# A feed-forward block and a long convolution on one core: which activation pairs take the seven-product path in both matrix products, when their buffers are lent, and how long the planner takes adding transfers to be

## The chip, the cores and the metric

The kernel runs on one core of one Trainium2 chip. The time is the device time of one execution in microseconds (us); the figure given for a kernel is the median of its runs. The engines of the core are PE (TensorE, matrix products), DVE (VectorE), ACT (ScalarE), POOL (GpSimd, here almost only an issuer of adding transfers) and SP (SyncE, which issues the other transfers). Each engine works through its own queue of instructions in the order in which they were written.

## The reference

Two branches read the same layer-normalised rows and are added to the input (S = 2048 rows, D = 1024, F = 3584; all float32):

```python
xn = _layernorm(x, axis=-1)                                  # x = A_q
# branch A: short causal convolution of k (4 taps), times v, then a long causal convolution by FFT
kv = k_shift * v
y  = irfft(rfft(pad(kv)) * rfft(pad(ssm_k)))[:S] + kv * ssm_D
A  = xn * y
# branch B: feed-forward
B  = silu(xn @ w1) @ w2
out = x + A + B
```

## The kernel before

Branch B is what PE mostly does. Each float32 factor is split into a high and a low float16 part and each product of blocks is made of three matmuls (high by high, high by low, low by high; lines 916 to 918 for the first matrix product, 1046 to 1048 for the second). The 3584 hidden columns are 28 blocks of 128, or 14 pairs (`NP`).

The first matrix product (`units`, line 952) uses a Strassen-Winograd scheme: for a pair and one half of the rows, seven products P1 to P7 of 12 matmuls take the place of eight. Such a unit is 84 matmuls. The first row half (`sp` = 0) has units for pairs 2 to 13, the second (`sp` = 1) for pairs 0 to 13; pairs 0 and 1 are done in plain form for the first half, before the units. PE shares four accumulators (`ff`) with the engines that empty them: in `evacuate` (line 879) PE has to wait until ACT has copied a running sum (P6 waits for the copy of P1's sum, P5 for that of P6's, P3 for that of P5's), and until DVE has added two of them into the low half (the two `v_tt` there, line 336 in the profile, `hf<-ff,hf`).

What follows on a unit depends on the pair. For the pairs that are not in `PAIRS`, `blocks` (line 841) splits the activation of each of two row blocks into float16 parts (one ACT and one DVE instruction of 1024 columns for each) and stores four transfers of 256 KB in `hs`. For the four pairs in `PAIRS`, `quad` (line 799) makes the seven sums and differences that the second matrix product needs for its own seven-product scheme: four `v_tt` of 512 columns on DVE, three splits of 1024 columns and one of 512 (ACT and DVE both), and seven stores of 256 KB in `hsf`. The split tiles live in `hts`, two tiles that can each be halved. The unsplit upper half of such a pair lives in `parts`, two places in the buffer `x4` that are kept until the row half's last quad is done (`room`, line 831).

The second matrix product adds up the ten plain pairs (`steps2`, for all 16 row tiles and two column halves, 1920 matmuls) and then the four pairs of `PAIRS` in `units2` (672 matmuls). Each result is copied or combined into a tile of `hfs` and sent out by POOL with a transfer that adds to `out` in memory (`G`, line 331).

Branch A, the convolution, goes on under all this in eight groups of 128 channels: DVE does most of it (a radix step, the product in the frequency domain, the inverse step; tiles `spec` and `tmp`), and once a group PE has a burst of 96 matmuls (tiles `ps`, lines 1494 to 1496 forward and 1686 to 1688 inverse). The result of a burst is gated into `yt` (or into `hts` or `wo` tiles), which POOL adds to `out` with `G`.

The order of the instructions on all engines is made by a list scheduler inside the kernel (`Order`, line 106). Each stream of work is a generator of `Op`s; each `Op` has an estimate `busy` of the time it holds its engine and `late` of the time until its result can be used. The scheduler always emits the op that can start first by these estimates, less a bias for its stream. For `G` the estimate is 1.1 us on POOL and 3.0 us more until the transfer has landed, which is when the tile it reads may be written again.

Once `flag["quads", 1]` is set (the second half's last quad has its last split), the `hts` tiles are not needed by branch B any more, and the convolution's streams may take them as further buffers (`parts_tile`, `signal_parts`, `parts_of`, `norm_rows`, `gated`).

Of the kernel before, what the change touches and what calls it, by code (L numbers as in the profile page):

```python
# [18 lines left out]
ADD, SUB, MUL = ALU.add, ALU.subtract, ALU.mult  # L19
# [10 lines left out]
NP = NF // 2  # L30
# [9 lines left out]
            "P5": ("S1", "T1"), "P3": ("S4", "B22"), "P4": ("A22", "T4")}  # L40
XPLACE = dict(A11=2, A12=3, A22=5, S1=0, S2=6, S3=7, S4=1)

PAIRS = (10, 11, 12, 13)
NQ = len(PAIRS)
PLAIN = [j for j in range(NF) if j // 2 not in PAIRS]
NC = len(PLAIN) // 4
# [59 lines left out]
class Order:  # L106
# [27 lines left out]
    def add(self, gen, bias, floor=0.0):  # L134
        s = Stream(gen, bias, floor)
        self.streams.append(s)
        self.advance(s)
# [151 lines left out]
def h3_ffn_kernel(ctx, tc, x, kp, vs, fs, shift, dskip, w1, w2, cfwd, cinv, out):  # L289
    nc = tc.nc  # L290
    ctx.enter_context(tc.manual_schedule())
    order = Order()
    add = order.add
    flag = defaultdict(Token)
# [12 lines left out]
    def size(a):  # L307
        n = 1
        for s in a.shape[1:]:
            n *= s  # L310
        return n
# [10 lines left out]
    def L(o, i, m=0.3):  # L322
        n = size(o) * o.shape[0] * mybir.dt.size(o.dtype)
        return Op("SP", 0.4, 0.1, lambda: nc.sync.dma_start(o, i), [i], [o], m, n)
# [5 lines left out]

    def G(o, i, m=0.3):
        n = size(i) * i.shape[0] * mybir.dt.size(i.dtype)
        return Op("POOL", 1.1, 3.0, lambda: nc.gpsimd.dma_start(o, i, accum_op=ADD), [i], [o], m, n)  # L333

    def v_tt(o, a, b, op, **k):
        return V(lambda: nc.vector.tensor_tensor(o, a, b, op=op), o, [a, b], **k)  # L336
# [20 lines left out]
    def split(hi, lo, src, scale, after=()):  # L357

        yield a_act(hi, src, AF.Copy, scale)
        yield v_stt(lo, src, scale, hi, MUL, SUB)  # L360
        for t in after:
            t.set()
# [39 lines left out]
    wo = Halves(order, wp, "wo", WO)  # L402
    hfs = Halves(order, wp, "hf", 3)
    vs_r = ws_r = hfs
    hts = Halves(order, wp, "ht", 2)
# [391 lines left out]
    quads = defaultdict(dict)  # L797

    def quad(i, sp):

        def factors(names, hf, toks=()):
            n = len(names)
            yield hts.ready if n == 1 else hts.pairs
            ht, ttok = (hts.tile if n == 1 else hts.pair)([P, 4 * n, 2, P], F16, n)
            yield from split(ht[:, :, 0], ht[:, :, 1], hf, wsc[:, i, 2:3], toks)
            for f, name in enumerate(names):
                yield L(hsf[sp][name][:, :, PAIRS.index(i)].rearrange("q p h s -> p q (h s)"),
                        ht[:, 4 * f:4 * f + 4].rearrange("p q h s -> p q (h s)"))
                ttok.set()

        yield flag["quad", i, 2 * sp]
        up, utok = quads[i, 2 * sp]
        flat = [up.rearrange("p j q s -> p (j q) s")]
        yield from factors(("A11", "A12"), flat[0])
        yield flag["quad", i, 2 * sp + 1]
        low, ltok = quads[i, 2 * sp + 1]
        flat.append(low.rearrange("p j q s -> p (j q) s"))
        x, y, z, v = up[:, 0], up[:, 1], low[:, 0], low[:, 1]
        yield from factors(("A22",), flat[1][:, 4:])
        yield v_tt(v, z, v, ADD)  # L820
        yield v_tt(z, x, z, SUB)
        add(factors(("S3", "S1"), flat[1], (ltok,)), 0.1)
        yield v_tt(x, v, x, SUB)
        ltok.set()
        yield v_tt(y, y, x, SUB)
        add(factors(("S2", "S4"), flat[0], (utok, flag["quads", sp])), 0.1)

    for sp in range(2):
        flag["quads", sp] = Token(NQ)

    def room():

        for sp in range(2):
            yield flag["room", sp]
            yield places[4].ready
            t, tok = places[4].tile([P, 2, 2 * W], F32)
            parts.open(t, 2)
            yield flag["quads", sp]
            tok.set()

    def blocks(i, b, hf, tok, ready):

        if i in PAIRS:
            return
        for r in ready:
            yield r
        yield hts.pairs
        ht, ttok = hts.pair([P, 8, 2, P], F16, 2)
        yield from split(ht[:, :, 0], ht[:, :, 1], hf.rearrange("p j q s -> p (j q) s"), wsc[:, i, 1:2], (tok,))
        for j in range(2):  # L850
            yield L(hs[b][:, :, 2 * i + j].rearrange("q p h s -> p q (h s)"),
                    ht[:, 4 * j:4 * j + 4].rearrange("p q h s -> p q (h s)"))
            ttok.set()

    def silu(i, o, src, tok, done):
        yield a_act(o, src, AF.Silu, wsc[:, i, 3:4])
# [6 lines left out]
    def places_of(i, b):  # L863

        made = Token(2)
        if i in PAIRS:
            r = hfs if b % 2 else parts
# [84 lines left out]
    def units():  # L952
# [5 lines left out]
        for n, (i, sp) in enumerate(todo):  # L958
            if sp == 1:
                flag["unit", i].set()  # L960
                flag["room", 1].set()
            if i in PAIRS:
                add(quad(i, sp), 0.1)
# [361 lines left out]
    def convolution(floor):  # L1325
# [3 lines left out]
        sp = ra.tile([P, 2, 8, 2, 2 * P], F32, name="spec")  # L1329

        def ring(name, bufs, pool=ra):
            return Ring(order, pool, name, bufs)

        kin_r, kf_r, acc_r, cm_r = (ring(*a) for a in (
            ("kin", 1), ("kf", 1), ("acc", 1), ("cm", 1)))
        hl_r = Halves(order, ra, "hl", 3)
# [90 lines left out]
        def parts_tile(hr, lr):  # L1427

            two = []
            for r in (hr, lr):  # L1430
                yield lambda: r.ready() or flag["quads", 1]() and hts.ready()
                two.append((r if r.ready() else hts).tile([P, 2, 2 * 2 * P], F16))
            return two

        def signal_parts():

            for g in range(NG):
                yield flag["scales", g]
                acc, atok = accs[g]
                for t in TO:  # L1440
                    yield lambda: cm_r.ready() or flag["quads", 1]() and hts.ready()
                    c, ctok = cpart[g, t] = (cm_r if cm_r.ready() else hts).tile([P, 2, 4, P], F16)
                    yield from split(c[:, 0], c[:, 1], slots(acc)[:, t::4], scs[g][0][:, 0:1], (flag["cpart", g, t],))
                atok.set()

        def parts_of():

            for g in range(NG):
                yield flag["scales", g]
                kf, ktok = kfs[g]  # L1450
                for t in TO:
                    yield lambda: hl_r.pairs() or flag["quads", 1]() and hts.pairs()
                    part[g, t] = x, _ = (hl_r if hl_r.pairs() else hts).pair([P, 2, 2, 4, P], F16)
                    done = flag["part", g, t]
                    done.n = 2
                    add(split(x[:, 1, 0], x[:, 1, 1], slots(kf)[:, t::4], scs[g][0][:, 1:2], (ktok, done)), CB)
                    yield flag["cpart", g, t]
                    c, ctok = cpart.pop((g, t))
                    yield X(x[:, 0].rearrange("p f s w -> p (f s) w"), c.rearrange("p f s w -> p (f s w)"))
                    ctok.set()  # L1460
                    done.set()
# [195 lines left out]
        def norm_rows():  # L1657

            for g in range(NG):
                for t in TO:  # L1660
                    r = more["xg"]
                    yield lambda: r.ready() or flag["quads", 1]() and hts.ready()
                    xgs[g, t] = xg, _ = (r if r.ready() else hts).tile([P, 2, 2, P])
                    for b in range(2):
                        yield L(xg[:, b], x4[b][:, :, t, g * P:(g + 1) * P])
                    for b in range(2):
                        for i in range(2):
                            n = b * T2 + 4 * i + t
                            yield a_act(xg[:, b, i], xg[:, b, i], AF.Identity, rstd[:, n:n + 1], nmr[:, n:n + 1])
                    flag["xg", g, t].set()  # L1670
# [23 lines left out]
        def gated(g, t, py, tok):  # L1694
            yield flag["xg", g, t]
            xg, xtok = xgs.pop((g, t))
            r = more["yt"]
            yield lambda: r.ready() or flag["quads", 1]() and hts.ready() or flag["h end"]() and wo.ready()
            r = wo if flag["h end"]() and wo.ready() else r if r.ready() else hts
            yt, ytok = r.tile([P, 2, 2, P], uses=2)  # L1700
            sc, stok = scs[g]
            flat = [q.rearrange("p b i w -> p (b i w)") for q in (yt, py, xg)]
            yield v_stt(flat[0], flat[1], sc[:, 5:6], flat[2], MUL, MUL)
            tok.set()
            xtok.set()
            if t == TO[-1]:
                stok.set()
            yield flag["copied", g // (NG // 2)]
            for b in range(2):
                yield G(out4[b][:, :, t, g * P:(g + 1) * P], yt[:, b])  # L1710
                ytok.set()
                if g < NG // 2:
                    flag["conv out"].set()
# [108 lines left out]
```

## Time and profile before

| | |
|---|---|
| median of 3 runs | 1261.48 us (1260.78 to 1261.53) |
| the profiled execution, its time | 1262.56 us |
| the profiled execution, its span | 1260.8 us |
| granted TensorE clock, mean | 0.992 |
| instructions in the span | 17032 |

The profile shows one execution. A row of a group reads: line, engine, operation, what it writes from what it reads (buffer numbers left out), shapes, how often, then busy time and mean duration, then how long the engine stood idle just before these instructions and which instruction ended that. A row of the timeline reads: start and duration in us, engine, line, operation, and in brackets the idle time before it with the instruction that ended it. In a row of a stretch stand its length and then, for each engine, the busy time and the number of instructions, then the granted clock, the mean busy share of the 16 transfer engines and the rate in GB/s.

### The profile page before, as it was taken

The page shows a single profiled execution, that of the slowest core. Times are in us where ns is not written, and L with a number is a line of the kernel's source. Part 1 is how long each engine was busy: PE and PEld are TensorE (multiplying, and loading weights), DVE is VectorE, ACT ScalarE, POOL GpSimd, SP SyncE. Part 2 cuts the span into 40 slices and gives each one's busy share as a digit, 9 for nine tenths or more (in the row PEclk, how much of TensorE's full clock was granted, in tenths as well). Part 3 has the DMA queues.
Part 4 walks back from the last instruction along what each step waited for, and adds up shares of the span by engine and source line. Part 5 has one row for each costly group of instructions (what it writes and reads, how often), then busy time and mean ns, then how long its engine had stood idle before and what let it go on. Part 6 is the DMA issues. An engine that isn't in the chain of part 4 may idle for free.

```text
span 1260.8 us, 17032 instructions
## 1 busy us (share of the span) xinstructions
PE 1233.3 (98%) x6018; PEld 596.5 (47%) x6018; DVE 1148.6 (91%) x1515; ACT 731.0 (58%) x1169; POOL 132.8 (11%) x141
## 2 busy tenths in 40 slices
PE   7899999999999999999999999999999999999997
PEld 6444554444444454444444544544444454445444
DVE  7999997898799979999999899989979989998995
ACT  6858897877866686667762442372263246536232
POOL 0000000000000030001110210120030021113114
PEclk7999999999999999999999999999999999999999
DMA  9358889879999799889998797599477578977767
GB/s 333 93 173 275 285 301 327 271 253 328 329 346 297 252 242 283 243 248 271 335 334 210 175 263 182 136 273 255 117 160 208 138 158 239 273 162 139 157 139 92
DMA packets 254181, 292.93 MB, mean 232 GB/s; under 512 B 48784, under 2 KB 167568, under 8 KB 251920
## 3 DMA queue, kind: packets, MB, share of 16 engines
q1 hardware_dynamic: 227360, 266.93, 67.9%
q0 software_dynamic: 26736, 24.92, 14.8%
q8 instruction: 47, 0.77, 0.2%
q14 instruction: 38, 0.31, 0.1%
HBM read 193.22 MB, written 98.57 MB: 231 GB/s over the span
## 4 chain that ended last, share of the span: by engine, by line
PE 63%; DVE 18%; DMA 3%; issue 3%; ACT 3%; POOL 0%; DVEq 0%; ACTq 0%
PE ff L1046 9%; PE ff L1048 9%; PE ff L1047 9%; PE ff L916 9%; PE ff L918 9%; PE ff L917 9%; DVE spec L336 7%; DVE tmp L336 3%; PE ps L1494 2%; PE ps L1496 2%; PE ps L1495 2%; DVE x L339 1%; DVE ht L339 1%; DVE acc L339 1%; DVE hf L336 1%
## 5 line engine op out<-in xcount | busy, mean ns | idle before, releaser
L1046 PE MATMUL ff<-x,wo 128*128 128x512 f16 x864 | 327.4, 379 | 1.2 <-ACT hf L347 0.8
L1048 PE MATMUL ff<-x,wo 128*128 128x512 f16 x864 | 327.4, 379 | 0.0
L1047 PE MATMUL ff<-x,wo 128*128 128x512 f16 x864 | 327.4, 379 | 0.0
L916 PE MATMUL ff<-x,wo 128*128 128x512 f16 (+1 forms) x808 | 305.6, 378 | 6.4 <-ACT x L347 2.2
L917 PE MATMUL ff<-x,wo 128*128 128x512 f16 (+1 forms) x808 | 305.4, 378 | 2.2 <-DVE x L339 2.2
L918 PE MATMUL ff<-x,wo 128*128 128x512 f16 (+1 forms) x808 | 305.5, 378 | 1.6 <-DVE wo L339 1.6
L336 DVE TENSOR_TENSOR spec<-spec 128x1024 f32<-128x1024 f32 (+2 forms) x272 | 263.5, 1000 | 2.8
L1048 PEld LDWEIGHTS <-wo 128*128 128x128 f16 x864 | 84.5, 98 | 101.9
L1046 PEld LDWEIGHTS <-wo 128*128 128x128 f16 x864 | 85.5, 99 | 99.5
L1047 PEld LDWEIGHTS <-wo 128*128 128x128 f16 x864 | 84.5, 98 | 101.2 <-issue 1.8
L918 PEld LDWEIGHTS <-wo 128*128 128x128 f16 x808 | 79.9, 99 | 98.0 <-issue 3.4
L917 PEld LDWEIGHTS <-wo 128*128 128x128 f16 x808 | 79.9, 99 | 95.2 <-issue 7.4
L916 PEld LDWEIGHTS <-wo 128*128 128x128 f16 x808 | 81.3, 101 | 89.3 <-ACT wo L347 1.0
L333 POOL DMA_DIRECT2D out<-hf x63 | 57.5, 917 | 458.8 <-ACT hf L347 402.9
L333 POOL DMA_DIRECT2D out<-yt x56 | 62.5, 1275 | 330.6 <-DVE yt L339 188.3
L347 ACT ACTIVATE hf<-ff,invc 128x512 f32<-128x512 f32 x64 | 43.4, 681 | 91.9 <-PE ff L1048 68.9
L336 DVE TENSOR_TENSOR tmp<-spec 128x2048 f32<-128x2048 f32 (+1 forms) x48 | 92.2, 1934 | 1.0
L347 ACT ACTIVATE spec<-spec 128x1024 bf16<-128x1024 f32 x32 | 33.8, 1055 | 92.4 <-DVE spec L336 92.4
L339 DVE SCALAR_TENSOR_TENSOR ht<-hf,wsc,ht 128x1024 f16<-128x1024 f32 (+1 forms) x56 | 67.3, 1203 | 10.9 <-ACT ht L347 10.9
L339 DVE SCALAR_TENSOR_TENSOR acc<-kin,taps,acc 128x1024 f32<-128x1024 f32 x48 | 61.5, 1280 | 11.9 <-ACT acc L347 11.6
L347 ACT ACTIVATE spec<-ps 128x512 f32<-128x512 f32 x96 | 54.9, 590 | 19.0 <-PE ps L1496 17.7
L347 ACT ACTIVATE ht<-hf,wsc 128x1024 f16<-128x1024 f32 (+1 forms) x56 | 60.9, 1088 | 5.0 <-DVE hf L336 1.4
(168 smaller groups left out, 1743.1 us busy)
## 6 DMA issues: line engine op xcount, KB each, us to landing
wo<-hs SPq DMA_DIRECT2D x160, 256.0 KB, 3.9
hs<-ht SPq DMA_DIRECT2D x80, 256.0 KB, 4.7
out<-hf POOLq DMA_DIRECT2D x63, 256.0 KB, 4.5
wraw<-in_w SPq DMA_DIRECT2D x30, 512.0 KB, 5.6
raw<-in_w SPq DMA_DIRECT2D x28, 512.0 KB, 5.5
kin<-in_kp SPq DMA_DIRECT2D x16, 704.0 KB, 6.1
kf<-in_fs SPq DMA_DIRECT2D x8, 1024.0 KB, 5.8
hl<-in_vs SPq DMA_DIRECT2D x32, 256.0 KB, 5.7
```

The costliest lines, as they stand in the source:

```text
L333: return Op("POOL", 1.1, 3.0, lambda: nc.gpsimd.dma_start(o, i, accum_op=ADD), [i], [o], m, n)
L336: return V(lambda: nc.vector.tensor_tensor(o, a, b, op=op), o, [a, b], **k)
L339: return V(lambda: nc.vector.scalar_tensor_tensor(o, a, s, b, op0=op0, op1=op1), o, [a, b] + ([] if isinstance(s, float) else [s]), **k)
L347: nc.scalar.activation(o, i, func, scale=scale, **kw)
L916: nc.tensor.matmul(o, w[:, 0, k], xf[:, :, k, 0], start=first and k == 0, stop=False, **kw)
L917: nc.tensor.matmul(o, w[:, 0, k], xf[:, :, k, 1], start=False, stop=False, **kw)
L918: nc.tensor.matmul(o, w[:, 1, k], xf[:, :, k, 0], start=False, stop=last and k == KH - 1, **kw)
L1046: nc.tensor.matmul(po, hx[:, n, 0, :], wc[:, n, 0, :], start=first and n == 0, stop=False, **kw)
L1047: nc.tensor.matmul(po, hx[:, n, 0, :], wc[:, n, 1, :], start=False, stop=False, **kw)
L1048: nc.tensor.matmul(po, hx[:, n, 1, :], wc[:, n, 0, :], start=False, stop=last and n == 3, **kw)
L1494: nc.tensor.matmul(o, cf[:, 0], hi[i], start=i == 0, stop=False, **kw)
L1495: nc.tensor.matmul(o, cf[:, 0], lo[i], start=False, stop=False, **kw)
```

## The change

Three edits. `PAIRS` becomes (8, 9, 12, 13), so pairs 8 and 9 take the seven-product path in both matrix products and pairs 10 and 11 go the plain way; `PLAIN` follows from it, and the fifth group of plain blocks in the second matrix product is pairs 10 and 11. A new token `flag["activations"]` counts every quad and every plain block (`2 * NQ + 4 * (NP - NQ)` of them); the five places that lent `hts` tiles on `flag["quads", 1]` wait for it. The estimate `late` of `G` goes from 3.0 to 4.8 us; it is a number of the planner and no instruction has it.

```diff
-PAIRS = (10, 11, 12, 13)
+PAIRS = (8, 9, 12, 13)
...
-        return Op("POOL", 1.1, 3.0, lambda: nc.gpsimd.dma_start(o, i, accum_op=ADD), [i], [o], m, n)
+        return Op("POOL", 1.1, 4.8, lambda: nc.gpsimd.dma_start(o, i, accum_op=ADD), [i], [o], m, n)
...
-        add(factors(("S2", "S4"), flat[0], (utok, flag["quads", sp])), 0.1)
+        add(factors(("S2", "S4"), flat[0], (utok, flag["quads", sp], flag["activations"])), 0.1)
...
+    flag["activations"] = Token(2 * NQ + 4 * (NP - NQ))
...
             ttok.set()
+        flag["activations"].set()
...
-                yield lambda: r.ready() or flag["quads", 1]() and hts.ready()
+                yield lambda: r.ready() or flag["activations"]() and hts.ready()
...
-                    yield lambda: cm_r.ready() or flag["quads", 1]() and hts.ready()
+                    yield lambda: cm_r.ready() or flag["activations"]() and hts.ready()
...
-                    yield lambda: hl_r.pairs() or flag["quads", 1]() and hts.pairs()
+                    yield lambda: hl_r.pairs() or flag["activations"]() and hts.pairs()
...
-                    yield lambda: r.ready() or flag["quads", 1]() and hts.ready()
+                    yield lambda: r.ready() or flag["activations"]() and hts.ready()
...
-            yield lambda: r.ready() or flag["quads", 1]() and hts.ready() or flag["h end"]() and wo.ready()
+            yield lambda: r.ready() or flag["activations"]() and hts.ready() or flag["h end"]() and wo.ready()
```

## The prediction

> **What bounds the kernel now.** The page's first part is read first, for the engine that could set the end.
>
> ```profile
> span 1260.8 us, 17032 instructions
> PE 1233.3 (98%) x6018; PEld 596.5 (47%) x6018; DVE 1148.6 (91%) x1515; ACT 731.0 (58%) x1169; POOL 132.8 (11%) x141
> ```
>
> PE is busy for 98% of the span, but a busy PE need not be at its pace, so the timeline comes next, where PE goes on after a stop.
>
> ```profile
> 589.85 0.38 PE L916 MATMUL ff<-x,wo 128*128 128x512 f16 x1 [2.02 <-ACT hf L347]
> ...
> 590.50 0.38 PE L916 MATMUL ff<-x,wo 128*128 128x512 f16 x1
> ```
>
> Two matmuls are left out between these, so the starts are 0.216 us apart (0.65 over three) although one lasts 0.38. Matmuls follow at this pace wherever nothing is waited for, so a unit of 84 takes 18.1 us, and the change leaves all of them in place. Only PE's stops can therefore be won or lost. The view of stretches of 30 us says where they are (the second number of a row is PE busy), and the view of waits says on whom.
>
> ```profile
> 0.00:30.00 30.00, 21.42 (x134) 17.93 (x135) 21.99 (x61) 17.93 (x40) 0.70 (x6) 0.81 0.96 347
> 30.00:60.00 30.00, 25.42 (x140) 14.56 (x139) 28.59 (x56) 27.68 (x45) 0.00 (x0) 0.90 0.34 101
> 330.00:360.00 30.00, 28.39 (x132) 12.83 (x131) 23.75 (x25) 24.27 (x39) 0.00 (x0) 1.00 1.04 328
> ```
>
> ```profile
> PE ff L916 <- ACT hf L347: 2.0, 1, 2.0
> PE ff L916 <- DVE hf L336: 1.6, 1, 1.6
> PE ps L1494 <- ACT spec L347: 1.6, 1, 1.6
> PE ps L1494 <- ACT tmp L347: 0.8, 1, 0.8
> PE ff L1046 <- ACT hf L347: 0.8, 1, 0.8
> PE ps L1494 <- DVE spec L336: 0.5, 1, 0.5
> PE ff L1046 <- DVE hf L339: 0.5, 1, 0.5
> PE ps L1687 <- DVE zl L339: 0.4, 1, 0.4
> PE ps L1494 <- DVE yt L339: 0.4, 1, 0.4
> ```
>
> The first 60 us lose 8.6 + 4.6 us, before any pair that changes sides. The nine waits above are all that is left until the tail, 8.6 us together. The 0.8 on `ACT hf` at L1046 is the last unit's, which has no next P1 to put between P5 and P3; it stays. So with no stop at all the kernel would be 7.8 us faster, about 1253.7, and everything the change can win is in these rows. What it can lose is in DVE, 91% busy, which feeds PE.
>
> **The change part by part.** *The pairs.* What a quad costs over a plain pair, for one row half:
>
> ```profile
> L339 DVE SCALAR_TENSOR_TENSOR ht<-hf,wsc,ht x56: 744/1278/1286, 41.2 to 612.0; 128x1024 f16<-128x1024 f32 x48, 128x512 f16<-128x512 f32 x8
> L336 DVE TENSOR_TENSOR hf<-hf x8: 681/685/693, 260.0 to 608.7; 128x512 f32<-128x512 f32 x8
> ```
>
> A quad has three splits of 1.278, one of 0.744 and four sums of 0.685: 7.3 us of DVE. A plain pair has two splits: 2.6. ACT has three and a half splits of 1024 columns against two. Seven stores of 256 KB stand against four, 0.79 MB more, which at the 328 GB/s of the stretch from 330 us is 2.4 us of transfers. Nothing is saved in sum, since as many pairs become plain; what moves is 4.8 us of DVE for each of two pairs in each row half, two units (some 36 us) earlier. Where these pairs stand is told by their stores:
>
> ```profile
> 273.83 1.62 SPq L324 DMA_DIRECT2D hsfA<-ht  x3
> 537.20 0.93 SPq L324 DMA_DIRECT2D hsfA<-ht  x2
> ```
>
> The first row is pair 11's in the first half, so pair 10's is some 20 us before it; the second is pair 10's in the second half. Pairs 8 and 9 thus get their quads at about 215 to 255 and 500 to 540 us, and pairs 12 and 13 stay behind two plain pairs at each end.
>
> ```profile
> 210.00:240.00 30.00, 30.00 (x142) 13.69 (x140) 23.51 (x32) 24.29 (x34) 0.95 (x1) 1.00 0.93 323
> 240.00:270.00 30.00, 30.00 (x143) 13.97 (x142) 26.73 (x43) 22.16 (x35) 0.00 (x0) 1.00 0.77 247
> 480.00:510.00 30.00, 30.00 (x141) 13.62 (x140) 29.79 (x30) 20.37 (x35) 0.00 (x0) 1.00 0.91 278
> 510.00:540.00 30.00, 30.00 (x142) 13.81 (x141) 29.31 (x39) 19.81 (x30) 0.00 (x0) 1.00 0.83 222
> ```
>
> In the first half 2 x 4.76 = 9.5 us of DVE meet 6.5 + 3.3 = 9.8 us of idle time, although one of the four old quads is still in these rows: hidden by DVE's own idle time, cost nothing. If that cover were gone, the price would be the next case's. In the second half DVE has 0.2 and 0.7 us to spare; 9.5 us more push the convolution's steps back by as much, which the 40 us from 540 on give back, where pairs 10 and 11 leave. Late next are the low-half sums `hf<-ff,hf` and then PE. Nothing in the trace shows two quads behind a burst, so the cost is bounded: below by nothing, since the first of today's quads begins in a stretch (510 to 540) where PE is at 30.00 of 30 with DVE as full; above by the largest stop of such a stretch, 2.02. I take **+0.5**, nearer to the lower end, because that stretch is the nearest row.
>
> *The stop at 332 us (1.6).* DVE's timeline around the last quad of the first half:
>
> ```profile
> 327.85 0.69 DVE L336 TENSOR_TENSOR hf<-x,hf 128x512 f32<-128x512 f32 x1
> 328.57 0.69 DVE L336 TENSOR_TENSOR x<-hf,x 128x512 f32<-128x512 f32 x1
> 329.30 0.69 DVE L336 TENSOR_TENSOR x<-x 128x512 f32<-128x512 f32 x1
> 329.90 1.28 DVE L339 SCALAR_TENSOR_TENSOR ht<-hf,wsc,ht 128x1024 f16<-128x1024 f32 x1
> 331.10 0.68 DVE L336 TENSOR_TENSOR spec<-spec,ps 128x512 f32<-128x512 f32 x1
> 331.70 0.68 DVE L336 TENSOR_TENSOR hf<-ff,hf 128x512 f32<-128x512 f32 x1
> ```
>
> The sum `hf<-ff,hf`, which PE waits for, stands behind three quad sums, a split and a convolution step, 4.0 us in which PE has 12 matmuls of the convolution, 2.6 us. In the order of the changed program pair 13's quad sums stand earlier: between the last of them and the corresponding `hf<-ff,hf` PE has 27 feed-forward matmuls (5.8 us), and DVE two splits and two steps of the convolution (2 x 1.28 + 2 x 0.68 = 3.9 us). I take the whole of it, **-1.6**; the other end is 0.
>
> *The stop at 589.85 (2.0).* Here ACT is late:
>
> ```profile
> 586.01 1.15 ACT L347 ACTIVATE ht<-x,wsc 128x1024 f16<-128x1024 f32 x1 [1.17 <-DVE ht L339]
> 587.06 0.67 ACT L347 ACTIVATE x<-ff,wsc 128x512 f32<-128x512 f32 x1
> ...
> 589.20 0.60 ACT L347 ACTIVATE hf<-ff 128x512 f32<-128x512 f32 x1
> ```
>
> A split of pair 12 waits 1.17 us for DVE to be done with an `ht` half, and the copy that PE needs is queued behind it. In the changed order the burst begins 24 feed-forward matmuls (5.2 us) earlier and lies in ten pieces of 3 to 21 matmuls instead of six with 39 in one of them, and that split stands 21 matmuls (4.5 us) ahead of the copy. The 1.17 us should go and most of the rest with it: **-1.6**, between 0 and -2.0.
>
> *The estimate for adding transfers.*
>
> ```profile
> out<-yt POOLq DMA_DIRECT2D x56, 128.0 KB, 6.2
> DVE yt L339 <- DMA out<-yt: 11.1, 9, 2.2
> 721.69 0.75 DVE L339 SCALAR_TENSOR_TENSOR yt<-ps,csc,ht 128x512 f32<-128x512 f32 x1 [1.00 <-DMA out<-yt]
> ```
>
> The planner put the landing at 1.1 + 3.0 = 4.1 us and now puts it at 5.9; the trace has 6.2 for `yt`. Because of that DVE was sent to a `yt` tile too early nine times and stood there for 11.1 us, with the sums behind it that empty PE's `ps`. Of the stops above only the 0.4 on `DVE yt` hangs on it plainly: **-0.4**, down to -1.1 if the 0.5 on `DVE spec` and a part of the 1.6, which lie in such a burst too, go with it; 0 if the tile is taken as early as before. The Trainium skill, in DMA: Bandwidth & Descriptors (Anatomy of one DMA — SWDGE (gpsimd) path), puts a transfer issued by GpSimd at about 2.0 us and its bytes over 436 GB/s; an estimate from that page for 128 KB is 2.3 us. By that rule the old constant already was too long and this edit could only delay work, a term of 0 in place of -0.4; the trace's 6.2 differs, and the measurement decides.
>
> *The token.* Pair 13 is the last unit in both kernels, and its last split fires both tokens: nothing moves, 0. If a plain block's split came after it, the lending would begin one split (1.28 us) later.
>
> The other stops (0.8 + 1.6 + 0.5 + 0.5 + 0.4) are in bursts of the second product, whose order in the changed program is the same with a start 9 to 18 matmuls earlier: 0. Sum: +0.5 - 1.6 - 1.6 - 0.4 = **-3.1 us**. The profiled execution took 1262.56, so 1259.5 for one like it; it lay 1.1 above the median, and from 1261.48 the forecast is **1258.4**.
>
> **The rivals.** *Given back (no change).* The stretches that lose their stop get one elsewhere. For it: three of the stops hang on tenths of a us of DVE or ACT, and every instruction after about 200 us is planned anew. Against it: the two large ones are in the quad stretches, which get lighter. Then the 3.1 is lost in two or three new stops of 1 to 1.6: about 1261.3.
>
> *The quads behind the burst in the second half (slower).* A burst runs from about 450 to 475 us, right ahead of pairs 8 and 9's units:
>
> ```profile
> 450.00:480.00 30.00, 30.00 (x153) 14.73 (x152) 25.40 (x27) 25.39 (x46) 9.13 (x9) 1.00 1.06 290
> ```
>
> ACT is at 25.4 of 30 and the transfers are full here, and DVE full after it. If the 9.5 us of quads go ahead of the low-half sums, PE stops in each of the two units as it did at 589.85, and the next burst starts with DVE late and stops once more as at 935: 2.0 + 2.0 + 2.1, less the 1.6 of the first half: +4.5, 1266.0. It decides as soon as DVE's queue ahead of one `hf<-ff,hf` is longer than the matmuls left before P5, 24 of them or 5.2 us; a quad's sums and two splits are 5.3. Against it: today's quads have that queue and passed.
>
> *The bursts mend too (faster).* With a true landing time the DVE no longer blocks in bursts: the 1.6, 0.8 and 0.5 go as well, -2.9 more: 1255.5. Against it: the 1.6 is ACT behind a load of `xg` rows, which the estimate doesn't touch.
>
> ```profile
> 934.95 0.49 ACT L347 ACTIVATE ht<-ht,nmr,rstd 128x128 f32<-128x128 f32 x1 [4.47 <-DMA ht<-in_x]
> ```
>
> **How the numbers follow.** Forecast 0.48, given back 0.17, slower 0.22, bursts mend 0.13. Some 0.2% (2.5 us) is what a measurement can tell from no change: faster is below 1259.0, slower above 1264.0. The forecast's own range, 1256.5 to 1260.5 from the bounds of its terms, lies two thirds below 1259.0: 0.32 + 0.13 = 0.45 for faster; its last third and the give-back are 0.16 + 0.17 = 0.33 for the same; 0.22 for slower. The range is 1254.5 to 1265.5: it leaves out some 0.04 of the mending case below and some 0.14 of the slower case above.
>
> **What would show it.** Right: no stop of PE over 1 us between 320 and 345 us or between 575 and 605; idle time of DVE on `out<-yt` well under 11.1 us; the stops in the bursts of the second product as before; PE busy at 30.0 of 30 from 480 to 540. Wrong: a wait of PE on `DVE hf` or `ACT hf` between 215 and 255 or 500 and 545 us, or new stops on `ps` in the bursts at about 450, 820 or 1030 us, which today have none.

## The result and the profile after

| | before | after |
|---|---|---|
| median | 1261.32 us, 6 runs (1259.08 to 1262.60) | 1255.76 us, 6 runs (1255.52 to 1256.82) |
| ratio, 95% interval | 1 | 0.9957 (0.9947 to 0.9967) |
| profiled span | 1260.8 us | 1254.2 us |
| PE's stops after the first 60 us, without the last unit's 0.8 | 7.8 us | 2.2 us |

The kernel became 5.6 us faster, 0.43%; 3.1 us had been forecast. The profile's first part and the busiest of its transfer rows, after:

```profile
span 1254.2 us, 17039 instructions
PE 1231.4 (98%) x6018; PEld 595.1 (47%) x6018; DVE 1146.5 (91%) x1515; ACT 731.4 (58%) x1169; POOL 132.7 (11%) x141
...
out<-hf POOLq DMA_DIRECT2D x63, 256.0 KB, 4.3
...
out<-yt POOLq DMA_DIRECT2D x56, 128.0 KB, 5.8
```

All five engines have the counts of before. The shares of busy time are the same too, so they say nothing about the gain. The view of waits says it. Here are DVE's wait for the adding transfers and all of PE's waits above 0.3 us after the first 60 us (waiting engine, tile and line, what it waited for, us in total, how often, the longest):

```profile
DVE yt L339 <- DMA out<-yt: 3.6, 4, 1.3
...
PE ps L1496 <- ACT tmp L347: 0.9, 1, 0.9
...
PE ff L1048 <- ACT hf L347: 0.8, 1, 0.8
...
PE ps L1496 <- DVE yt L339: 0.7, 1, 0.7
PE ff L918 <- ACT hf L347: 0.6, 1, 0.6
```

The row of L1048 is the last unit's 0.8. The other three of PE make 2.2 us where before had 7.8. The difference, 5.6, equals the gain between the medians only by chance: a profile is of one execution, and the two profiled spans differ by 6.6 (the profiled execution of before was 1.2 above its median, that of the changed kernel 0.2). Taken between the starts of matmuls, as in the table further down, the stops are 6.5 us less, nearly all of the 6.6 between the spans. The stretches of 30 us show the two large stops gone, and PE undisturbed where the new quads are:

```profile
210.00:240.00 30.00, 30.00 (x142) 13.81 (x141) 26.04 (x37) 24.75 (x34) 0.95 (x1) 1.00 0.99 328
330.00:360.00 30.00, 30.00 (x141) 13.62 (x139) 27.69 (x28) 21.96 (x37) 0.00 (x0) 1.00 1.00 338
480.00:510.00 30.00, 30.00 (x142) 13.83 (x141) 29.73 (x38) 21.33 (x36) 0.00 (x0) 1.00 0.89 274
510.00:540.00 30.00, 30.00 (x141) 13.62 (x140) 29.88 (x36) 20.87 (x30) 0.00 (x0) 1.00 0.89 269
570.00:600.00 30.00, 29.96 (x163) 15.80 (x162) 26.44 (x31) 24.83 (x38) 7.02 (x7) 1.00 0.93 254
```

From 330 us PE is busy for 30.00 of 30 (28.39 before), from 570 for 29.96. At 210 us DVE has 26.04 in place of 23.51: part of a quad that used to come later. From 510 us it has 29.88, only 0.12 us of idle time left, and PE goes on at 30.00 all the same.

DVE's timeline at 327 us shows what was taken away in front of the sum that PE waited for. The bracket is the idle time before the instruction:

```profile
327.38 1.28 DVE L339 SCALAR_TENSOR_TENSOR ht<-hf,wsc,ht 128x1024 f16<-128x1024 f32 x1 [4.25 <-ACT ht L347]
328.58 1.28 DVE L339 SCALAR_TENSOR_TENSOR ht<-x,wsc,ht 128x1024 f16<-128x1024 f32 x1
329.77 0.68 DVE L336 TENSOR_TENSOR hf<-ff,hf 128x512 f32<-128x512 f32 x1
```

Two splits stand ahead of `hf<-ff,hf`; before it was three sums of a quad, a split and a step of the convolution, with no idle time. Now DVE had 4.25 us to spare ahead of them. ACT's timeline at the place of the second large stop:

```profile
583.20 0.60 ACT L347 ACTIVATE hf<-ff 128x512 f32<-128x512 f32 x1
585.68 1.15 ACT L347 ACTIVATE ht<-x,wsc 128x1024 f16<-128x1024 f32 x1 [1.88 <-DMA hsfA<-ht]
```

A split still waits, and longer than before (1.88 us for a store, against 1.17 for DVE). But it stands behind the copy `hf<-ff`, and no later copy that PE needs is held up by it. The wait was not removed; it was put where nobody waits for it.

Of the three stops that remain, the 0.9 on `ACT tmp`, at 702.76 us, is the 0.8 that before had at 708.30, ahead of the same burst. Two are new: the 0.7 on `DVE yt` at 817 us, where DVE stood 1.3 us for an adding transfer, and one at 404 us. All engines around that one:

```profile
402.23 1.06 ACT L347 ACTIVATE yt<-yt 128x1024 f32<-128x1024 f32 x1 [3.35 <-DMA yt<-in_w]
...
403.28 0.58 ACT L347 ACTIVATE hf<-ff 128x512 f32<-128x512 f32 x1
...
403.92 0.38 PE L918 MATMUL ff<-x,wo 128*128 128x512 f16 x1 [0.58 <-ACT hf L347]
```

ACT stands at a `yt` that a transfer has not filled yet, 3.35 us long, and the copy for PE is queued behind it: a stop of the old kind, at a new place, for other data.

### The profile page after: what moved, and what is told of

It is laid out like the page before. It is cut to its first block, busy times and chain, and to the rows that moved or that the text cites. A ratio compares the mean times of both kernels' runs of the same rounds, so it can differ in the third digit from the quotient of the medians.

```text
span 1254.2 us, 17039 instructions
## 1 busy us (share of the span) xinstructions
PE 1231.4 (98%) x6018; PEld 595.1 (47%) x6018; DVE 1146.5 (91%) x1515; ACT 731.4 (58%) x1169; POOL 132.7 (11%) x141
## 4 chain that ended last, share of the span: by engine, by line
PE 72%; DVE 9%; DMA 4%; issue 2%; ACT 1%; POOL 0%; SPq 0%; DVEq 0%; ACTq 0%; POOLq 0%
PE ff L1048 12%; PE ff L1050 12%; PE ff L1049 12%; PE ff L918 9%; PE ff L919 9%; PE ff L920 9%; DVE spec L336 3%; PE ps L1496 2%; PE ps L1497 2%; PE ps L1498 2%; DVE x L339 1%; DVE tmp L336 1%; DVE spec L339 1%; PE ps L1690 1%; PE ps L1688 1%
## 5 line engine op out<-in xcount | busy, mean ns | idle before, releaser
L1048 PE MATMUL ff<-x,wo 128*128 128x512 f16 x864 | 327.4, 379 | 0.8 <-ACT hf L347 0.8
L1048 PEld LDWEIGHTS <-wo 128*128 128x128 f16 x864 | 85.4, 99 | 99.6
```

The costliest lines, as they stand in the source:

```text
L1048: nc.tensor.matmul(po, hx[:, n, 0, :], wc[:, n, 0, :], start=first and n == 0, stop=False, **kw)
```

## The experiments

Two kernels take the edits apart. The other ten ask a second question: how much of a difference of some tenths of a per cent is the edit, and how much is that every instruction is planned anew? For them one number of the planner that belongs to neither edit, the rate at which it assumes transfers to pass, is moved by one part in 330, and by 2, 3 and 4. No instruction has it; it changes the order, and with it which buffer an instruction takes. It is done to the kernel before and to the changed one alike.

In the table, "stops" are the distances between starts of matmuls over their pace, each above 0.3 us and after the first 60 us, the last unit's 0.9 included; each is 0.1 to 0.2 longer than its row among the waits. "Rest" is the profiled span less the stops.

| kernel | median us (least to most, runs) | ratio, 95% interval | span | stops | rest | DVE waits on `out<-yt` |
|---|---|---|---|---|---|---|
| before | 1261.32 (1259.08–1262.60, 6) | 1 | 1260.8 | 10.4 | 1250.4 | 11.1, 9 times |
| after | 1255.76 (1255.52–1256.82, 6) | 0.9957 (0.9947–0.9967) | 1254.2 | 3.9 | 1250.3 | 3.6, 4 |
| e1, pairs only | 1265.50 (1260.95–1271.31, 12) | 1.0037 (1.0021–1.0053) | 1261.5 | 10.6 | 1250.9 | 10.5, 7 |
| e2, estimate only | 1261.58 (1259.89–1265.27, 12) | 1.0000 (0.9988–1.0012) | 1258.1 | 6.7 | 1251.3 | 3.5, 4 |
| e3, before, 331 | 1256.53 (1255.09–1258.92, 7) | 0.9962 (0.9948–0.9976) | 1254.0 | 4.4 | 1249.5 | 4.7, 4 |
| e4, after, 331 | 1264.89 (1262.11–1266.70, 11) | 1.0021 (1.0009–1.0033) | 1263.6 | 12.5 | 1251.1 | 10.1, 4 |
| e5, before, 329 | 1262.38 (1261.02–1265.86, 10) | 1.0016 (1.0004–1.0028) | 1260.5 | 10.4 | 1250.1 | 8.8, 6 |
| e6, after, 329 | 1259.12 (1257.23–1260.31, 10) | 0.9985 (0.9975–0.9995) | 1256.5 | 6.5 | 1250.1 | 2.4, 3 |
| e7, before, 332 | 1261.14 (1258.80–1264.46, 10) | 1.0001 (0.9989–1.0014) | 1260.1 | 9.3 | 1250.8 | 6.0, 4 |
| e8, after, 332 | 1258.84 (1258.08–1260.63, 10) | 0.9981 (0.9972–0.9991) | 1256.8 | 6.1 | 1250.8 | 5.1, 5 |
| e9, before, 333 | 1263.59 (1259.55–1269.11, 10) | 1.0033 (1.0014–1.0052) | 1259.6 | 9.8 | 1249.8 | 12.0, 7 |
| e10, after, 333 | 1262.96 (1262.24–1265.81, 10) | 1.0021 (1.0011–1.0030) | 1260.9 | 9.6 | 1251.3 | 1.2, 2 |
| e11, before, 334 | 1266.49 (1260.79–1269.10, 10) | 1.0035 (1.0020–1.0049) | 1260.9 | 11.0 | 1249.9 | 13.0, 7 |
| e12, after, 334 | 1262.08 (1260.36–1265.85, 10) | 1.0018 (1.0008–1.0028) | 1261.5 | 12.2 | 1249.3 | 2.8, 2 |

Each ratio is against runs of before beside it (medians of 1260.7 to 1261.6); it is worked out from all these runs and can differ by 0.1% from the quotient of the medians. Span, stops, rest and waits are of one execution. In e1, e9 and e11 that execution was 2.2, 2.2 and 3.5 us under the median, so the stops shown do not account for those medians. The outputs of e3, e4, e7 and e12 are wrong, with a relative error of 0.07 (why is open, see the end). Every engine's count of instructions in their traces is that of the others and all 127 adding transfers to `out` are there, so their times are given; but a plan with a wrong output is no kernel to be used, and what rests on these four is weaker for it.

**e1: the pairs alone.** The estimate stays at 3.0.

```diff
-PAIRS = (10, 11, 12, 13)
+PAIRS = (8, 9, 12, 13)
```

> The kernel before with PAIRS = (8, 9, 12, 13) alone, the estimate of G at 3.0. Theory (two edits, two kinds of stop): the stops at the quads (1.6 on DVE hf near 332 us and 2.0 on ACT hf near 590 us) are gone, the idle time of DVE on out<-yt stays near 11 us, and the bursts of the second product keep stops of 3 to 4 us in sum: ratio 0.997, some 1257.7 us. Rival (the estimate does it all): 1260 to 1262, both quad stops stay. Rival (a draw of the planner): anything from 1254 to 1264, with stops in places that neither edit names.

Measured: 0.37% slower than before; the profiled execution, 2.2 us under the median, is only 0.7 longer than that of before. DVE's wait on the adding transfers and PE's waits:

```profile
DVE yt L339 <- DMA out<-yt: 10.5, 7, 4.7
...
PE ps L1494 <- ACT spec L347: 2.7, 1, 2.7
...
PE ps L1494 <- ACT tmp L347: 2.2, 2, 1.5
PE ps L1494 <- DVE yt L339: 1.9, 2, 1.5
...
PE ff L1046 <- ACT ff L347: 0.9, 1, 0.9
```

Neither the stop at 332 nor that at 590 is there, as in the changed kernel, and the 11.1 us of DVE's waits stay at 10.5. But the other stops come to 7.7 us (2.7 + 2.2 + 1.9 + 0.9) where before had 4.2. Of the 1.9 on `DVE yt`, 1.5 are in the burst at 452 us, ahead of the new quads; the rest of the 7.7 is after 700 us. The largest of them, in the timeline:

```profile
1036.28 1.06 ACT L347 ACTIVATE hl<-kf 128x1024 bf16<-128x1024 f32 x1 [4.94 <-DMA kf<-in_dskip]
...
1039.41 1.06 ACT L347 ACTIVATE spec<-ps 128x512 f32<-128x512 f32 x2
...
1040.52 0.38 PE L1494 MATMUL ps<-hl,cfw 128*128 128x512 f16 x1 [2.70 <-ACT spec L347]
```

ACT waits 4.94 us for a load, and the copies of `ps` are behind it. That place is in the second product, some 400 us after the last quad. In this plan the edit of the pairs does what it says at its own place, and what it wins there is lost elsewhere.

**e2: the estimate alone.** The pairs stay 10 to 13.

```diff
-        return Op("POOL", 1.1, 3.0, lambda: nc.gpsimd.dma_start(o, i, accum_op=ADD), [i], [o], m, n)
+        return Op("POOL", 1.1, 4.8, lambda: nc.gpsimd.dma_start(o, i, accum_op=ADD), [i], [o], m, n)
```

> The kernel before with the estimate of G at 4.8 alone, PAIRS = (10, 11, 12, 13). Theory: DVE's idle time on out<-yt falls from 11.1 to 3 to 5 us, the stops of PE in the bursts near 715 and 935 us shrink by 1.5 to 2.5 us, the stops at the quads stay at 1 to 2 us each: ratio 0.998 to 0.999, some 1259.5 us. Rival (the pairs do it all): no change, 1261, with 935 us still at 2 us. Rival (a draw): anything from 1254 to 1264.

Measured: the time of before, 1.0000. Its waits:

```profile
DVE yt L339 <- DMA out<-yt: 3.5, 4, 1.3
...
PE ff L1046 <- ACT hf L347: 2.0, 2, 1.2
...
PE ff L916 <- DVE hf L336: 1.6, 1, 1.6
...
PE ff L916 <- ACT hf L347: 0.8, 1, 0.8
PE ps L1494 <- DVE yt L339: 0.7, 1, 0.7
...
PE ps L1494 <- ACT tmp L347: 0.3, 1, 0.3
```

DVE's waits do what was expected: its idle time on `out<-yt` falls from 11.1 to 3.5 us, and the stops at 936 and 1143 us are gone. The stop at 332 is there with its 1.6. The one at 590 is 0.8 in place of 2.0, though no pair has moved. In the bursts 2.2 us remain (1.2 + 0.7 + 0.3) of 4.2, the 1.2 of them new at 1094. In this execution the waits are 3.2 us less than before (4.6 against 7.8); it was the fastest of its twelve, so the median shows nothing.

The parts do not add up: +0.37% and 0.00% alone, -0.43% together. If each edit had an effect of its own that adds to the other's, this could not be. The token is left out of the sum: with the token alone the program has the same instructions, order and waits as before, and without it the changed program is the same too, so it wasn't run.

**e3 and e4: the same two kernels with another plan.** The edit, in the planner's account of transfers, first in the kernel before, then in the changed one:

```diff
-                self.pipe = max(self.pipe, t + 3.0) + op.nbytes / 330e3
+                self.pipe = max(self.pipe, t + 3.0) + op.nbytes / 331e3
```

> The kernel before with one number of the planner changed that stands for nothing in the change: its transfer rate is 331 in place of 330 GB/s, so the order is planned anew with the same pairs and the same estimate of G. Theory (the two edits remove causes): the time stays within 2 us of before, 1259.5 to 1263, with stops at the quads and in the bursts of 6 to 10 us in sum. Rival (a draw): it moves by 3 us or more, either way, as the change did.

> The changed kernel with the same neutral number, 331 in place of 330 GB/s. Theory: it stays at 1254.5 to 1257.5 us, with no stop over 1 us at the quads and DVE's idle time on out<-yt under 6 us. Rival (a draw): it goes back to 1259 or more.

Measured: the signs change places. The kernel before, with neither edit, becomes 0.38% faster, nearly as much as by the whole change; the changed kernel, with both, becomes 0.21% slower than before. PE's waits in e3:

```profile
PE ps L1494 <- DVE tmp L336: 0.8, 1, 0.8
PE ff L1046 <- ACT hf L347: 0.8, 1, 0.8
PE ps L1494 <- ACT spec L347: 0.6, 1, 0.6
PE ps L1494 <- ACT tmp L347: 0.5, 1, 0.5
...
PE ps L1494 <- DVE yt L339: 0.3, 1, 0.3
```

No wait on `DVE hf` is left: the stop at 332, which the edit of the pairs was to remove, is gone with pairs 10 to 13 in their places. In e4 PE's waits are these, and ACT's timeline at the largest:

```profile
PE ff L1048 <- ACT ff L347: 3.0, 1, 3.0
...
PE ps L1496 <- ACT tmp L347: 2.3, 2, 1.6
...
PE ps L1496 <- DVE yt L339: 1.8, 4, 1.0
```

```profile
1093.01 0.72 ACT L347 ACTIVATE x<-wraw,tau 128x512 f16<-128x512 f32 x1 [2.19 <-DMA wraw<-in_w]
...
1093.63 0.58 ACT L347 ACTIVATE ff<-ff 128x512 f32<-128x512 f32 x1
```

Again ACT waits for a load (2.19 us), a copy that PE needs is behind it, and the place, in the second product, belongs to neither edit. (Both outputs are among the wrong ones.)

**e5 to e12: four more plans of each.** The edit is the same line with 329e3, 332e3, 333e3 and 334e3.

> The kernel before planned anew by the neutral number 329 in place of 330 GB/s. Theory after the first four runs (a stop hangs on the plan, and each plan draws its own): 1255 to 1265, with stops of 4 to 12 us after the first 60 us, and the span equals 1251 plus these stops to within 1.5 us. Rival (the edits still shift the mean): the plans with (10, 11, 12, 13) and 3.0 lie at 1259 or more in most draws, this one too.

> The changed kernel planned anew by 329 in place of 330 GB/s. Theory (a draw): 1255 to 1265, as likely above the kernel before as below. Rival (the edits shift the mean): under 1259.

> The kernel before planned anew by 332 in place of 330 GB/s. Theory (a draw): 1255 to 1265. Rival (the edits shift the mean): 1259 or more.

> The changed kernel planned anew by 332 in place of 330 GB/s. Theory (a draw): 1255 to 1265. Rival (the edits shift the mean): under 1259.

> The kernel before planned anew by 333 in place of 330 GB/s. Theory (a draw around a small shift: so far the four plans of before lie at 1256.5 to 1262.4, mean 1260.3, the four of the changed kernel at 1255.8 to 1264.9, mean 1259.7): 1256 to 1264, and the span is 1249.5 to 1251.5 plus the stops after the first 60 us. DVE's idle time on out<-yt 5 to 11 us. Rival (the edits shift the mean by 3 us or more): 1260 or more.

> The changed kernel planned anew by 333 in place of 330 GB/s. Theory (a draw): 1255 to 1264, span 1249.5 to 1251.5 plus the stops; no stop at 332 us, as in none of the plans with (8, 9, 12, 13); DVE's idle time on out<-yt 2 to 6 us. Rival (the edits shift the mean by 3 us or more): under 1258.

> The kernel before planned anew by 334 in place of 330 GB/s. Theory (a draw): 1256 to 1264, span 1249.5 to 1251.5 plus the stops. Rival (the edits shift the mean): 1260 or more.

> The changed kernel planned anew by 334 in place of 330 GB/s. Theory (a draw): 1255 to 1264, no stop at 332 us, span 1249.5 to 1251.5 plus the stops. Rival (the edits shift the mean): under 1258.

Measured: at 329, 332, 333 and 334 the changed kernel has the lower ratio, by 0.31, 0.20, 0.12 and 0.17%, though at the last three the intervals of the two overlap. At 331 it has the higher one by 0.59, and at 330, the kernels of this case, the lower one by 0.43. Over six plans each, the mean ratio of the kernel before is 1.0008 and that of the changed kernel 0.9997, with a standard deviation of 0.0027 among the plans of either. The difference of the means is -0.11%, with a standard error of 0.16% (0.0027 times the root of 2/6). With only the four plans of each whose output is right (330, 329, 333 of both, 334 of before, 332 of the changed one) the means are 1.0021 and 0.9986: -0.35%, with the same standard error. So neither no effect of the edits nor the whole 0.43% is excluded. What is shown is that the plan alone moves a kernel by as much as the change did: the changed kernel's plans with a right output go from 0.9957 to 1.0021.

e5 tells how far a single profile can be trusted. Its program has the order of before on all engines, except between 340 and 440 us and between 650 and 680 us. Yet its waits of PE are not the same:

```profile
PE ps L1494 <- DVE yt L339: 2.8, 3, 1.8
...
PE ps L1494 <- ACT tmp L347: 1.3, 2, 0.8
...
PE ff L916 <- ACT hf L347: 1.1, 1, 1.1
```

Before had 0.4, 0.8 and 2.0 in these rows. The stop near 590 us, the 1.1, is about half as long, and after 680 us the waits above 0.3 come to 4.7 us, in part at other instructions, where before had 4.2. So a stop can differ by about 1 us between two profiles with the same order of instructions around it, and since each kernel has one profile, a smaller difference between two of them is not shown to come from the plan. It also means that e5 is hardly a new plan, so that there are five rather than six of the kernel before.

One of them, e12, shows the slower rival at work. DVE's and PE's timeline:

```profile
531.02 0.68 DVE L336 TENSOR_TENSOR x<-hf,x 128x512 f32<-128x512 f32 x1
...
531.73 0.69 DVE L336 TENSOR_TENSOR x<-x 128x512 f32<-128x512 f32 x1
...
532.34 1.28 DVE L339 SCALAR_TENSOR_TENSOR ht<-hf,wsc,ht 128x1024 f16<-128x1024 f32 x1
...
533.54 0.74 DVE L339 SCALAR_TENSOR_TENSOR cm<-acc,csc,cm 128x512 f16<-128x512 f32 x1
...
534.20 0.68 DVE L336 TENSOR_TENSOR hf<-ff,hf 128x512 f32<-128x512 f32 x1
...
534.94 0.38 PE L918 MATMUL ff<-x,wo 128*128 128x512 f16 x1 [2.67 <-DVE hf L336]
```

Two sums of a quad, a split and a step stand ahead of `hf<-ff,hf` without a gap, and PE stops for 2.67 us. It is the kind of stop that before had at 332 us, now at the pairs' new place.

## Why the prediction was right, and where it was not

**Only PE's stops count: shown.** In all fourteen profiled executions the span less the stops lies between 1249.3 and 1251.3 us, while the stops go from 3.9 to 12.5. Whatever else the plans change, the span of an execution is this constant, to within 2 us, and the stops.

**The stop at 332, -1.6: it came, by the mechanism named.** The row of 327.38 shows the sums of the quad gone from in front of `hf<-ff,hf`. A stop of 1 us or more stands there in 4 of the 7 plans with pairs 10 to 13 (before, e2, e5, e11) and in none of the 7 with the new pairs, where the largest is 0.5 in e12. So the pairs seem to bear on it, but e3, e7 and e9 lose it without them.

**The stop at 589.85, -1.6: it came with -2.0 in this plan; that the pairs remove it has not held up.** Between 575 and 605 us the stops of all kinds add up in the seven plans with the old pairs to 2.2, 1.0, 1.0, 1.2, 1.7, 1.3 and 1.6 us. With the new pairs three plans have 0, 0 and 0.5, but e4 has 2.4, e6 1.4, e10 1.5 and e12 3.5. In the changed kernel the split's wait itself stayed (1.88 us); what took the stop away there was the order, and other plans order it otherwise. That the size came so near is luck: the stop was 2.0 in before's profile and 1.1 in e5's, with the same order there.

**The new quads, +0.5: nothing here, but about the size over plans.** The prediction's cover, PE's 30.00 from 480 to 540, held. Over the seven plans with the new pairs the stops between 500 and 545 us are 0, 0.3, 1.1, 0.3, 0, 0 and 3.4, some 0.7 on the mean, against 0.2 with the old pairs (0.5 in e9 and 0.8 in e11). The rival's price of 2 us for each unit was right where it happens (2.67 in e12), and it happens in two plans of seven (e4 with 1.1 and e12), against the 0.22 given to it.

**The estimate, -0.4: the mechanism shown, and the 0.4 on `DVE yt` not won.** DVE's idle time on `out<-yt` is 9.4 us on the mean of the seven plans with 3.0 and 4.1 with 4.8 (one of them, e4, has 10.1). PE's wait on `DVE yt` hardly moves: 1.6 on the mean against 1.2, and 0.4 to 0.7 in this case. The Trainium skill, in DMA: Bandwidth & Descriptors (Anatomy of one DMA — SWDGE (gpsimd) path), would have had the old constant too long already, by the prediction's estimate of 2.3 us from it. The landing in the changed kernel is 5.8 us, and the fall of DVE's waits speaks for planning with the measured one.

**The other burst stops, 0: this is the step that failed.** The prediction put it as: "are in bursts of the second product, whose order in the changed program is the same with a start 9 to 18 matmuls earlier: 0". Together with the 0.4 on `DVE yt` they fell from 4.2 to 1.6, -2.6 where -0.4 had been counted. With the -2.0 in place of -1.6 at 590, the 0.5 not lost to the quads and 0.6 for the new stop at 404, that is the way from the forecast's terms to the waits of the two profiles: -1.6 - 2.0 - 2.6 + 0.6 = -5.6. The reading of the order was wrong. Most pieces of PE's bursts do come 12 to 18 matmuls earlier, but in the first four bursts of the second product the last six matmuls come 30 to 33 earlier, and the burst near 1147 us, which before is in six pieces of 6 to 21, is in five, one of them of 39. Nor would the same order have meant the same stops, as e5 shows. What decides is which wait of ACT or DVE stands in front of a copy that PE needs, and how long that wait is in the execution: the stops outside the quads' two places come to 4.2 us before, 4.7 in e5, 7.7 in e1, 2.2 in e2 and 1.6 after, the one at 404 us not counted.

This is the rival named "the bursts mend too", 1255.5, and its time is right to 0.3 us; with plans that differ by 0.27%, or 3.4 us, that nearness is luck. Its cause is shown in part: e2 has the stops at 936 and 1143 us gone with the estimate alone. That the true landing time mends bursts in general isn't: e4, planned with 4.8, loses about 6 us after 800 us (3.0 + 2.3 in its rows and some more).

**The signs named beforehand.** Those for the large stops, for DVE's idle time and for PE from 480 to 540 us came as said. Two did not: the stops in the bursts of the second product were to be as before, and they fell; and a new stop on `ps` at about 820 us, named as a sign of being wrong, is there with 0.7 us.

**The range.** The forecast's own range, 1256.5 to 1260.5, was given as that of the bounds of its terms; they add up to 1256.8 to 1263.5 (-1.6, -2.0 and -1.1 at one end, +2.02 at the other). The measured 1255.76 lies below both. It is inside the stated range because that left room for the rival that mends the bursts.

**What the prediction left out.** It treated each term as belonging to its edit, and gave 0.17 to new stops from the plan alone. The re-planning is no side effect here: a number that stands in no instruction moved the kernel before by -0.38% to +0.35%, and the changed kernel from 0.9957 to 1.0021. The direction was the forecast one in this plan and in four of the five others tried, by 0.12 to 0.31%, and the reverse in one. How much of the 0.43% the edits would keep over many plans stays open.

## What to carry to other kernels

Where one engine is busy for 98% and a planner sets the order of the rest, first list the busy engine's stops: here span less stops was the same within 2 us in fourteen programs, so a change was worth the stops that it took away. Before a gain of less than half a per cent is put down to an edit, move a neutral number of the planner by a few parts in a thousand in both kernels: the spread of those plans (0.27% here) is the yardstick, not the spread of the runs of one program. And read what stands in front of a stop: in the stops opened here the copy or sum that PE needed stood behind other work, or behind an instruction that itself waited for a load, a store or another engine, and the two largest of before went when that order changed.

## What was not expected of the hardware

The runs of one program agree better in some plans than in others. Among the plans with ten or more runs, those with the estimate of 3.0 spread over 4.8 to 10.4 us (10.4 in e1, 9.6 in e9, 8.3 in e11) and those with 4.8 over 2.6 to 5.5. A planner that takes transfers to land too early leaves more waits whose length is the transfer's own; that this is the cause wasn't tried. (The 31 runs of before beside each group spread over 6.0 to 7.6 us.)

Four of the ten plans with a new rate gave a wrong output (0.0686 in e3, 0.0697 in e4, e7 and e12), though they hold the same adding transfers. Two of these under way at once on the same part of `out` would be the first suspicion. By their issue and landing in the fourteen traces that did not happen: the nearest two on the same part are 0.35 us apart in e4, from the landing of one to the issue of the next, and 0.37 in e1, whose output is right. What was lost, and why, stays open.
